# Small fp32 products of a retention layer in four quarters of TensorE, with PSUM taken in pairs of banks

## The chip, the cores and the metric

One core of one Trainium2 chip. The metric is the device time of one execution in microseconds (us), the median of several runs.

## The reference, cut to what matters

```python
# q, k, v: (4, 8, 768, 64) fp32;  w_in: (512, 2048), w_out: (2048, 512) fp64
for t in range(S):                                   # retention, per head
    state = gamma * state + k_t (outer) v_t          # 64 x 64 for each of 32 heads
    y[t] = scale * q_t @ state
x = y, heads side by side                            # (3072, 512)
h = x @ w_in;  g = h * sigmoid(h);  out = g @ w_out  # (3072, 512)
```

The kernel works in six chunks c of 128 steps for each of four batches b. One pair (c, b) is a unit, and there are 24. Inside a chunk, y is the sum of two products: masked scores times v, and q times the state that the chunks before left.

Of the kernel before, what the change touches and what calls it, by code (L numbers as in the profile page):

```python
# [12 lines left out]
FP32 = mybir.dt.float32  # L13
FP32R = mybir.dt.float32r
U32 = mybir.dt.uint32
AF = mybir.ActivationFunctionType
ALU = mybir.AluOpType
# [8 lines left out]
EPS = 2.0 ** -12  # L26
# [5 lines left out]
def kernel(  # L32
# [21 lines left out]



    nc = tc.nc
    B, H, S, D = q.shape
    DM, DF = moe_w_in.shape
    C = 128  # L60
    NC = S // C
    HP = H // 2
    KIN = DM // 128
    NF = DF // 128
    NT = B * C
# [7 lines left out]
    PS = bass.MemoryType.PSUM  # L73

    def pool(name, bufs, **kw):
        return ctx.enter_context(tc.tile_pool(name=name, bufs=bufs, **kw))
# [3 lines left out]
    xpool = pool("xpool", 2)  # L80
    const = pool("const", 1)
    ld = pool("ld", 2)
    one = pool("one", 1)
    hpool = pool("hpool", 3)
    stage = pool("stage", 2)
    conv = pool("conv", 1)
    ps_a = pool("ps_a", 4, space=PS)
    ps_h = pool("ps_h", 2, space=PS)

    g_dram = {(c, f): dram.tile([128, NT], FP32, tag=f"g{c}_{f}", name=f"gd_{c}_{f}")  # L90
# [23 lines left out]
    kqv = {"k": {}, "q": {}, "v": {}}  # L114
# [10 lines left out]



    staged = {}

    def load_w(i):  # L130
        if i >= 2 * NF:
            return
        if wide:
            t = stage.tile([128, 2 * DM], U32, tag="wf", name=f"wf_{i}")
            w_in, w_out, n = moe_w_in.bitcast(U32), moe_w_out.bitcast(U32), 256
        else:
            t = stage.tile([128, DM], FP32, tag="wf", name=f"wf_{i}")
            w_in, w_out, n = moe_w_in, moe_w_out, 128
        if i < NF:
            nc.sync.dma_start(out=t.rearrange("p (i f) -> p i f", i=KIN),  # L140
                              in_=w_in[:, ts(i, n)].rearrange("(i p) f -> p i f", p=128))
        else:
            nc.sync.dma_start(out=t, in_=w_out[ts(i - NF, 128), :])
        staged[i] = t
# [38 lines left out]
    evac, w_sb = [], {}  # L183
# [23 lines left out]
    ident = const.tile([128, 128], FP32, tag="ident", name="ident")  # L207
# [7 lines left out]
    decay = const.tile([128, 2, HP, C], FP32, tag="decay", name="decay")  # L215
# [40 lines left out]

    xt, kt, qt, am, live = {}, {}, {}, {}, {}

    def bank(name):
        return ps_a.tile([128, 512], FP32, tag="a", name=name)  # L260

    def scale_k(n):
        if 0 <= n < len(units) and units[n][0] < NC - 1:
# [9 lines left out]

    def stage_t(n):

        for name, src, to, bufs in (("k", kqv["k"][n], kt, 2), ("q", kqv["q"].pop(n), qt, 3)):
            tp = bank(f"{name}tp_{n}").rearrange("p (a t) -> p a t", a=HP)
            for a in range(HP):
                nc.tensor.transpose(tp[:, a, :], src[:, 2 * a : 2 * a + 2, :], ident)
            t = one.tile([128, HP, C], FP32, tag=f"{name}t", name=f"{name}t_{n}", bufs=bufs)  # L280
            evac[:] = [nc.scalar.copy(out=t, in_=tp).ins]
            to[n] = t

    def stage_a(n):

        ap = [bank(f"sc{j}_{n}").rearrange("p (a t) -> p a t", a=HP) for j in range(2)]
        ktn = kt.pop(n)
        for a in range(HP):
            for j in range(2):
                nc.tensor.matmul(ap[j][:, a, :], lhsT=ktn[ts(j, D), a, :],  # L290
                                 rhs=qt[n][ts(j, D), a, :], start=True, stop=True,
                                 skip_group_check=True)
        am[n] = []
        for j in range(2):
            t = one.tile([128, HP, C], FP32, tag=f"am{j}", name=f"am{j}_{n}")
            nc.vector.tensor_tensor(out=t, in0=ap[j], in1=decay[:, j], op=ALU.mult)  # L296
            am[n].append(t)

    def stage_y(n):

        c, b = units[n]
        kf, vs = kqv["k"].pop(n), kqv["v"].pop(n)
        qtn, amn = qt.pop(n), am.pop(n)
        if c < NC - 1:
            sp = bank(f"s_{n}")[:, : HP * D].rearrange("p (a e) -> p a e", a=HP)
            for a in range(HP):
                for j in range(2):
                    h = 2 * a + j
                    nc.tensor.matmul(sp[ts(j, D), a, :], lhsT=kf[:, h, :], rhs=vs[:, h, :],
                                     start=True, stop=True, skip_group_check=True)  # L310
        if b == 0 and c != LATE:
            xt[c] = xpool.tile([128, 3, KIN, NT], FP32R, tag="xt", name=f"xt_{c}")
        yp = bank(f"y_{n}").rearrange("p (a t) -> p a t", a=HP)

        if c > 0:
            for a in range(HP):
                for j in range(2):
                    nc.tensor.matmul(yp[ts(j, D), a, :], lhsT=state[b][ts(j, D), a, :],  # L318
                                     rhs=qtn[ts(j, D), a, :], start=(a == 0), stop=False,
                                     skip_group_check=True)  # L320
        for a in range(HP):
            for j in range(2):
                nc.tensor.matmul(yp[ts(j, D), a, :], lhsT=vs[:, 2 * a + j, :],  # L323
                                 rhs=amn[j][:, a, :], start=(c == 0 and a == 0), stop=True,
                                 skip_group_check=True)
        live[n] = sp if c < NC - 1 else None, yp

    def finish_y(n):
        c, b = units[n]
        sp, yp = live.pop(n)  # L330
        if c == LATE:
            y = hpool.tile([128, KIN, C], FP32, tag="hs", name=f"ys_{b}")
            nc.scalar.copy(out=y, in_=yp)
            nc.sync.dma_start(out=y_dram[b], in_=y)
        else:
            split_x(c, b, yp)
        if c == 0:
            nc.scalar.copy(out=state[b], in_=sp)
        elif c < NC - 1:
            nc.vector.tensor_tensor(out=state[b], in0=state[b], in1=sp, op=ALU.add)  # L340

    def split_x(c, b, y):
        xh, xl, xm = (xt[c][:, i, :, ts(b, C)] for i in range(3))
        nc.scalar.activation(out=xh, in_=y, func=AF.Copy, scale=HALF)
        nc.vector.tensor_tensor(out=xl, in0=y, in1=xh.bitcast(FP32), op=ALU.subtract)  # L345
        nc.vector.scalar_tensor_tensor(out=xm, in0=xl.bitcast(FP32), scalar=-1.0 / EPS,
                                       in1=xh.bitcast(FP32), op0=ALU.mult, op1=ALU.add)


    LATE = 2  # L350

    def late_x(b):
        if b == 0:
            xt[LATE] = xpool.tile([128, 3, KIN, NT], FP32R, tag="xt", name=f"xt_{LATE}")
        y = hpool.tile([128, KIN, C], FP32, tag="hs", name=f"yr_{b}")
        nc.sync.dma_start(out=y, in_=y_dram[b])
        split_x(LATE, b, y)

    visits = [0]

    def visit():
        m = visits[0]
        visits[0] += 1
        if m - 2 >= len(units):
            return
        if m < len(units):
            stage_t(m)
        if m >= 2:
            stage_y(m - 2)
        if 1 <= m <= len(units):  # L370
            stage_a(m - 1)
            scale_q(m - 1)
            scale_k(m - 1)
        if m >= 2:
            finish_y(m - 2)
        load("k", m + 2)
        load("q", m + 2)
        load("v", m)
# [77 lines left out]
    half = NF // 2  # L456
# [36 lines left out]
    for c in range(NC):  # L493
        acc = []
        for b in range(B):
            if b < 2:
                acc.append([bank(f"o{i}{b}_{c}") for i in "ab"])
            else:
                acc.append([ps_h.tile([128, DM], FP32, tag=f"h{i}", name=f"o{i}{b}_{c}")
                            for i in "ab"])  # L500
        for f in range(NF):
            n = c * NF + f
            split(n + S_AHEAD)
            t = ready.pop(n)
            first_, last = f == 0, f == NF - 1
            for b in range(B):
                gh, glo, gm = (t[:, i, ts(b, C)] for i in range(3))
                oa, ob = acc[b]
                nc.tensor.matmul(oa, lhsT=gh, rhs=wo[f][:, 0, :], start=first_, stop=False)  # L509
                nc.tensor.matmul(oa, lhsT=glo, rhs=wo[f][:, 1, :], start=False, stop=last)  # L510
                nc.tensor.matmul(ob, lhsT=gm, rhs=wo[f][:, 2, :], start=first_, stop=last)  # L511
        for b in range(B):
            oa, ob = acc[b]
            o = one.tile([128, DM], FP32, tag=("am0", "am1", "kt", "qt")[b], name=f"o_{c}_{b}",
                         bufs=(1, 1, 2, 3)[b])
            nc.scalar.activation(out=o, in_=oa, func=AF.Copy, scale=ONE_E)  # L516
            nc.vector.tensor_tensor(out=o, in0=o, in1=ob, op=ALU.subtract)  # L517
            nc.scalar.dma_start(out=out[ds(b * S + c * C, C), :], in_=o)
# [30 lines left out]
```

## The kernel before: the parts that the change and the argument touch

A *visit* is the retention work of one round: transposes of unit m, the products into y of unit m-2, the scores of unit m-1. Visits stand between the dense products (`ha`, `hb`) in TensorE's fixed order. The order of the other engines is not fixed by the program: the build picks it, and it also puts in the waits between instructions that touch the same tile. (The *build* turns the program into one list of instructions for each engine. *Masking* is VectorE's product of the scores with the decay. An *evacuation* is any reading of PSUM by ScalarE or VectorE that frees it for the next use.)

```python
ps_a = pool("ps_a", 4, space=PS)      # four single PSUM banks, taken in turn
ps_h = pool("ps_h", 2, space=PS)      # ha and hb, two each: the other four banks
...
def stage_t(n):                       # transposes; one bank for k, one for q
    for name, src, to, bufs in (("k", ...), ("q", ...)):
        tp = bank(f"{name}tp_{n}").rearrange("p (a t) -> p a t", a=HP)
        for a in range(HP):
            nc.tensor.transpose(tp[:, a, :], src[:, 2 * a : 2 * a + 2, :], ident)
        t = one.tile([128, HP, C], FP32, ...)
        evac[:] = [nc.scalar.copy(out=t, in_=tp).ins]
...
def stage_a(n):                       # scores: 64 rows by 128 columns, a bank for each j
    for a in range(HP):
        for j in range(2):
            nc.tensor.matmul(ap[j][:, a, :], lhsT=ktn[ts(j, D), a, :],
                             rhs=qt[n][ts(j, D), a, :], ...)
    for j in range(2):
        nc.vector.tensor_tensor(out=t, in0=ap[j], in1=decay[:, j], op=ALU.mult)
...
def stage_y(n):                       # s, then y of the state (64x64), then y of the scores (128x64)
    ...
        nc.tensor.matmul(sp[ts(j, D), a, :], lhsT=kf[:, h, :], rhs=vs[:, h, :], ...)
    ...
        nc.tensor.matmul(yp[ts(j, D), a, :], lhsT=state[b][ts(j, D), a, :],
                         rhs=qtn[ts(j, D), a, :], ...)
    ...
        nc.tensor.matmul(yp[ts(j, D), a, :], lhsT=vs[:, 2 * a + j, :], rhs=amn[j][:, a, :], ...)
...
def split_x(c, b, y):                 # the three parts of x: xh (ScalarE), xl and xm (VectorE)
...
def visit():
    stage_t(m); stage_y(m - 2); stage_a(m - 1); scale_q(m - 1); scale_k(m - 1); finish_y(m - 2)
```

## Time and profile before

| | before |
|---|---|
| median of 3 runs | 663.93 us |
| span of the profiled run | 661.2 us |
| TensorE, VectorE, ScalarE busy | 97%, 64%, 43% |
| one full late visit | 4.72 us |
| first late visit starts at | 173.0 us, 488.2 us before the end |

Two more lines are needed later. The first is VectorE's row of busy tenths, in 40 slices of 16.5 us; the second is a wait: who waited for whom, us in total, times, longest.

```profile
DVE  5999999985668677673447776364464554554631
...
PE qtp L279 <- DVE xt L345: 3.2, 3, 1.5
```

VectorE is full from the second slice to the eighth. In all the run, q's transposes waited three times for an evacuation of PSUM, and k's transposes not once. So four single banks, each let go by itself, were nearly enough.

### The profile page before, as it was taken

How to read it: one execution, taken by the hardware profiler on the slowest of the kernel's cores; microseconds unless marked ns; L12 is line 12 of the kernel's file. 1: busy time of each engine (PE TensorE's matmuls, PEld its weight loads, DVE VectorE, ACT ScalarE, POOL GpSimd, SP SyncE). 2: the span in 40 equal slices, each digit the busy share in tenths (PEclk: the TensorE clock that was granted, in tenths of full speed). 3: DMA queues.
4: the chain of work that ended last, by engine and by line, in shares of the span. 5: the costliest groups of instructions: out<-in, count | busy, mean ns of one | idle time of the engine just before them, and what ended most of it. 6: DMA issues, size and time to landing. Idle time of an engine off the chain costs nothing.

```text
span 661.2 us, 10308 instructions
## 1 busy us (share of the span) xinstructions
PE 639.6 (97%) x3904; PEld 525.1 (79%) x3904; DVE 424.1 (64%) x720; ACT 285.2 (43%) x510; POOL 11.1 (2%) x44
## 2 busy tenths in 40 slices
PE   4799999999999999999999999999999999999996
PEld 3578878876888888888888888888888888888885
DVE  5999999985668677673447776364464554554631
ACT  6565566645444544444447882222141312222311
POOL 3000000000000000000000000000000000000000
PEclk9999999999999999999999999999999999999999
DMA  9988878666557575754425754252343342423501
GB/s 224 207 176 200 212 211 223 208 219 210 159 153 216 180 219 160 223 168 152 128 81 160 214 184 143 65 178 80 125 131 124 121 134 85 170 86 105 160 0 64
DMA packets 122546, 103.45 MB, mean 156 GB/s; under 512 B 79488, under 2 KB 87680, under 8 KB 122496
## 3 DMA queue, kind: packets, MB, share of 16 engines
q1 hardware_dynamic: 119040, 96.49, 50.9%
q10 hardware_dynamic: 3456, 6.29, 2.6%
q8 instruction: 31, 0.51, 0.3%
q14 instruction: 19, 0.16, 0.1%
HBM read 66.06 MB, written 36.70 MB: 155 GB/s over the span
## 4 chain that ended last, share of the span: by engine, by line
PE 78%; DVE 14%; DMA 4%; issue 2%; ACT 1%; SPq 0%; DVEq 0%; ACTq 0%
PE ob L511 13%; PE oa L510 13%; PE oa L509 13%; PE ha L390 10%; PE hb L392 10%; PE ha L391 10%; PE y L323 2%; PE y L318 2%; PE sc L290 2%; DVE am L296 2%; DVE g L395 2%; DVE cp L177 1%; DVE wil L105 1%; DVE cs L173 1%; DMA vf<-in_v_dram 1%
## 5 line engine op out<-in xcount | busy, mean ns | idle before, releaser
L390 PE MATMUL ha<-xt,wi 128*128 128x512 f32 x384 | 152.2, 396 | 0.8 <-ACT g L394 0.8
L392 PE MATMUL hb<-xt,wi 128*128 128x512 f32 x384 | 150.3, 391 | 1.2 <-DVE g L395 0.8
L391 PE MATMUL ha<-xt,wi 128*128 128x512 f32 x384 | 149.8, 390 | 0.1
L511 PE MATMUL ob<-wo,gs 128*128 128x512 f32 x384 | 149.5, 389 | 0.0
L510 PE MATMUL oa<-wo,gs 128*128 128x512 f32 x384 | 149.4, 389 | 0.0
L509 PE MATMUL oa<-wo,gs 128*128 128x512 f32 x384 | 149.4, 389 | 0.0
L437 DVE TENSOR_TENSOR gs<-gr,gs 128x512 fp32r<-128x512 f32 x96 | 62.5, 686 | 92.5 <-ACT gs L435 92.5
L435 ACT ACTIVATE gs<-gr 128x512 fp32r<-128x512 f32 x96 | 53.5, 622 | 140.0 <-issue 129.6
L395 DVE TENSOR_TENSOR g<-g,hb 128x512 f32<-128x512 f32 x96 | 65.8, 685 | 67.0 <-ACT g L394 67.0
L392 PEld LDWEIGHTS hb<-xt,wi 128*128 128x128 f32 x384 | 72.1, 188 | 19.0 <-DVE g L395 3.1
L390 PEld LDWEIGHTS ha<-xt,wi 128*128 128x128 f32 x384 | 72.0, 188 | 18.8 <-ACT g L394 2.1
L394 ACT ACTIVATE g<-ha 128x512 f32<-128x512 f32 x96 | 57.1, 595 | 66.9 <-PE ha L391 62.0
L511 PEld LDWEIGHTS ob<-wo,gs 128*128 128x128 f32 x384 | 72.1, 188 | 15.8 <-DVE o L517 0.9
L510 PEld LDWEIGHTS oa<-wo,gs 128*128 128x128 f32 x384 | 72.1, 188 | 15.1
L391 PEld LDWEIGHTS ha<-xt,wi 128*128 128x128 f32 x384 | 72.1, 188 | 14.7 <-DVE xt L345 0.4
L396 ACT ACTIVATE g<-g 128x512 f32<-128x512 f32 x96 | 61.0, 636 | 52.7 <-DVE g L395 52.7
L509 PEld LDWEIGHTS oa<-wo,gs 128*128 128x128 f32 x384 | 72.1, 188 | 14.6
L438 DVE SCALAR_TENSOR_TENSOR gs<-gs 128x512 fp32r<-128x512 f32 x96 | 62.4, 686 | 0.4
L517 DVE TENSOR_TENSOR o<-o,ob 128x512 f32<-128x512 f32 x24 | 15.9, 687 | 38.9 <-ACT o L516 38.9
L516 ACT ACTIVATE o<-oa 128x512 f32<-128x512 f32 x24 | 13.7, 597 | 56.4 <-PE oa L510 49.1
L296 DVE TENSOR_TENSOR am<-sc,decay 128x512 f32<-128x512 f32 x48 | 31.5, 685 | 1.6 <-PE sc L290 1.6
L290 PE MATMUL sc<-qt,kt 64*128 64x128 f32 x384 | 28.6, 290 | 0.0
(59 smaller groups left out, 537.4 us busy)
## 6 DMA issues: line engine op xcount, KB each, us to landing
gd<-g SPq DMA_DIRECT2D x96, 256.0 KB, 3.0
gr<-gd SPq DMA_DIRECT2D x96, 256.0 KB, 2.7
wf<-in_moe_w_in_dram SPq DMA_DIRECT2D x16, 512.0 KB, 4.3
wf<-in_moe_w_out_dram SPq DMA_DIRECT2D x16, 512.0 KB, 3.9
kf<-in_k_dram SPq DMA_DIRECT2D x24, 256.0 KB, 4.7
qf<-in_q_dram SPq DMA_DIRECT2D x24, 256.0 KB, 5.0
vf<-in_v_dram SPq DMA_DIRECT2D x24, 256.0 KB, 4.1
out_dram<-o ACTq DMA_DIRECT2D x24, 256.0 KB, 2.1
```

The source lines that it names most:

```text
L390: nc.tensor.matmul(ha, lhsT=w[0], rhs=x[0], start=first_, stop=False)
L391: nc.tensor.matmul(ha, lhsT=w[1], rhs=x[1], start=False, stop=last)
L392: nc.tensor.matmul(hb, lhsT=w[2], rhs=x[2], start=first_, stop=last)
L394: nc.scalar.activation(out=hs, in_=ha, func=AF.Copy, scale=ONE_E)
L395: nc.vector.tensor_tensor(out=hs, in0=hs, in1=hb, op=ALU.subtract)
L396: nc.scalar.activation(out=hs, in_=hs, func=AF.Silu)
L435: nc.scalar.activation(out=t[:, 0, :], in_=g, func=AF.Copy, scale=HALF)
L437: nc.vector.tensor_tensor(out=t[:, 1, :], in0=g, in1=high, op=ALU.subtract)
L438: nc.vector.scalar_tensor_tensor(out=t[:, 2, :], in0=t[:, 1, :].bitcast(FP32), scalar=-1.0 / EPS, in1=high, op0=ALU.mult, op1=ALU.add)
L509: nc.tensor.matmul(oa, lhsT=gh, rhs=wo[f][:, 0, :], start=first_, stop=False)
L510: nc.tensor.matmul(oa, lhsT=glo, rhs=wo[f][:, 1, :], start=False, stop=last)
L511: nc.tensor.matmul(ob, lhsT=gm, rhs=wo[f][:, 2, :], start=first_, stop=last)
```

## The change

Its intent: fill all four 64 by 64 quarters of the array in the product of q and the state, and keep the array in one shape for as long as possible. For that it

- issues s, y of the scores, y of the state, scores, in that order, so that equal shapes are neighbours;
- sends the odd head pairs of y to the crossed quarters and to a second bank. This exchanges halves of x, so the rows of the first weights are loaded exchanged too, in three transfers in place of one;
- computes the scores as twice as many 64 by 64 products;
- takes PSUM in pairs of banks. Two pairs, in place of four single banks, serve in turn: a pair for k's and q's transposes, the next for y and s, the next for the scores, which are then masked by one VectorE operation of 1024. The accumulators and result buffers of the output stage follow suit;
- splits y ahead of the masking in the program, and makes the third part of x (`xm`) after it.

```diff
-    ps_a = pool("ps_a", 4, space=PS)
+    ps_u = pool("ps_u", 2, space=PS)
...
+            nc.sync.dma_start(out=to[0], in_=src[0])
+            for j in range(2):
+                nc.sync.dma_start(out=to[1, ts(j, D)], in_=src[1, ts(1 - j, D)])
...
+    def banks(name):
+        return ps_u.tile([128, 2, 512], FP32, tag="u", name=name)
...
     def stage_t(n):
-        for name, src, to, bufs in (("k", kqv["k"][n], kt, 2), ("q", kqv["q"].pop(n), qt, 3)):
-            tp = bank(f"{name}tp_{n}").rearrange("p (a t) -> p a t", a=HP)
+        tp = banks(f"tp_{n}")
+        for i, (name, src, to, bufs) in enumerate((("k", kqv["k"][n], kt, 2),
+                                                   ("q", kqv["q"].pop(n), qt, 3))):
+            part = tp[:, i].rearrange("p (a t) -> p a t", a=HP)
             for a in range(HP):
-                nc.tensor.transpose(tp[:, a, :], src[:, 2 * a : 2 * a + 2, :], ident)
+                nc.tensor.transpose(part[:, a, :], src[:, 2 * a : 2 * a + 2, :], ident)
             t = one.tile([128, HP, C], FP32, tag=f"{name}t", name=f"{name}t_{n}", bufs=bufs)
-            evac[:] = [nc.scalar.copy(out=t, in_=tp).ins]
+            evac[:] = [nc.scalar.copy(out=t, in_=part).ins]
...
+        for a in range(HP):                                # y of the scores, now first
+            for j in range(2):
+                o = j ^ (a % 2)
+                product(o, a % 2, out=yp[ts(o, D), a // 2, a % 2, :], ...)
+        if c > 0:                                          # y of the state, four quarters
+            for i in range(0, HP, 2):
+                for a in (i, i + 1):
+                    for j in range(2):
+                        o = j ^ (a % 2)
+                        product(o, a % 2, out=yp[ts(o, D), a // 2, a % 2, :],
+                                lhsT=state[b][ts(j, D), a, :], rhs=qtn[ts(j, D), a, :], stop=True)
...
+                for half in range(2):                      # scores in four quarters
+                    nc.tensor.matmul(u[ts(half, D), j, a, :], lhsT=ktn[ts(j, D), a, ts(half, D)], ...)
...
         if m >= 2:
             stage_y(m - 2)
+            rest = finish_y(m - 2)
         if 1 <= m <= len(units):
             stage_a(m - 1)
             scale_q(m - 1)
             scale_k(m - 1)
-        if m >= 2:
-            finish_y(m - 2)
+        if rest is not None:
+            rest()                                         # xm
```

More of the change, by code (lines that the diff above doesn't have):

```diff
@@ L139, in load_w @@
         if i < NF:
-            nc.sync.dma_start(out=t.rearrange("p (i f) -> p i f", i=KIN),
-                              in_=w_in[:, ts(i, n)].rearrange("(i p) f -> p i f", p=128))
+            to = t.rearrange("p (i o f) -> o p i f", o=2, f=n)
+            src = w_in[:, ts(i, n)].rearrange("(i o p) f -> o p i f", o=2, p=128)
+            nc.sync.dma_start(out=to[0], in_=src[0])
+            for j in range(2):
+                nc.sync.dma_start(out=to[1, ts(j, D)], in_=src[1, ts(1 - j, D)])
         else:
@@ L257 @@
     xt, kt, qt, am, live = {}, {}, {}, {}, {}
-    def bank(name):
-        return ps_a.tile([128, 512], FP32, tag="a", name=name)
+    def banks(name):
+        return ps_u.tile([128, 2, 512], FP32, tag="u", name=name)
     def scale_k(n):
@@ L280, in stage_t, with stage_y, product @@
             t = one.tile([128, HP, C], FP32, tag=f"{name}t", name=f"{name}t_{n}", bufs=bufs)
-            evac[:] = [nc.scalar.copy(out=t, in_=tp).ins]
+            evac[:] = [nc.scalar.copy(out=t, in_=part).ins]
             to[n] = t
+    def stage_y(n):
+        c, b = units[n]
+        kf, vs = kqv["k"].pop(n), kqv["v"].pop(n)
+        qtn, amn = qt[n], am.pop(n)
+        u = banks(f"y_{n}")
+        yp = u[:, :, : 2 * C].rearrange("p o (i t) -> p i o t", i=2)
+        sp = u[:, 1, 2 * C :].rearrange("p (a e) -> p a e", a=HP)
+        started = set()
+        def product(j, bank, **kw):
+            nc.tensor.matmul(start=(j, bank) not in started, skip_group_check=True, **kw)
+            started.add((j, bank))
+        if c < NC - 1:
+            for a in range(HP):
+                for j in range(2):
+                    h = 2 * a + j
+                    product(j, 1, out=sp[ts(j, D), a, :], lhsT=kf[:, h, :], rhs=vs[:, h, :],
+                            stop=True)
+        for a in range(HP):
+            for j in range(2):
+                o = j ^ (a % 2)
+                product(o, a % 2, out=yp[ts(o, D), a // 2, a % 2, :], lhsT=vs[:, 2 * a + j, :],
+                        rhs=amn[:, j, a, :], stop=(c == 0))
+        if c > 0:
+            for i in range(0, HP, 2):
+                for a in (i, i + 1):
+                    for j in range(2):
+                        o = j ^ (a % 2)
+                        product(o, a % 2, out=yp[ts(o, D), a // 2, a % 2, :],
+                                lhsT=state[b][ts(j, D), a, :], rhs=qtn[ts(j, D), a, :],
+                                stop=True)
+        live[n] = sp, yp
@@ L284, in stage_a @@
     def stage_a(n):
-        ap = [bank(f"sc{j}_{n}").rearrange("p (a t) -> p a t", a=HP) for j in range(2)]
+        u = banks(f"sc_{n}").rearrange("p j (a t) -> p j a t", a=HP)
         ktn = kt.pop(n)
@@ L289, in stage_a @@
             for j in range(2):
-                nc.tensor.matmul(ap[j][:, a, :], lhsT=ktn[ts(j, D), a, :],
-                                 rhs=qt[n][ts(j, D), a, :], start=True, stop=True,
-                                 skip_group_check=True)
-        am[n] = []
-        for j in range(2):
-            t = one.tile([128, HP, C], FP32, tag=f"am{j}", name=f"am{j}_{n}")
-            nc.vector.tensor_tensor(out=t, in0=ap[j], in1=decay[:, j], op=ALU.mult)
-            am[n].append(t)
-    def stage_y(n):
-        c, b = units[n]
-        kf, vs = kqv["k"].pop(n), kqv["v"].pop(n)
-        qtn, amn = qt.pop(n), am.pop(n)
-        if c < NC - 1:
-            sp = bank(f"s_{n}")[:, : HP * D].rearrange("p (a e) -> p a e", a=HP)
-            for a in range(HP):
-                for j in range(2):
-                    h = 2 * a + j
-                    nc.tensor.matmul(sp[ts(j, D), a, :], lhsT=kf[:, h, :], rhs=vs[:, h, :],
-                                     start=True, stop=True, skip_group_check=True)
-        if b == 0 and c != LATE:
-            xt[c] = xpool.tile([128, 3, KIN, NT], FP32R, tag="xt", name=f"xt_{c}")
-        yp = bank(f"y_{n}").rearrange("p (a t) -> p a t", a=HP)
-        if c > 0:
-            for a in range(HP):
-                for j in range(2):
-                    nc.tensor.matmul(yp[ts(j, D), a, :], lhsT=state[b][ts(j, D), a, :],
-                                     rhs=qtn[ts(j, D), a, :], start=(a == 0), stop=False,
-                                     skip_group_check=True)
-        for a in range(HP):
-            for j in range(2):
-                nc.tensor.matmul(yp[ts(j, D), a, :], lhsT=vs[:, 2 * a + j, :],
-                                 rhs=amn[j][:, a, :], start=(c == 0 and a == 0), stop=True,
-                                 skip_group_check=True)
-        live[n] = sp if c < NC - 1 else None, yp
+                for half in range(2):
+                    nc.tensor.matmul(u[ts(half, D), j, a, :], lhsT=ktn[ts(j, D), a, ts(half, D)],
+                                     rhs=qt[n][ts(j, D), a, :], start=True, stop=True,
+                                     skip_group_check=True)
+        am[n] = one.tile([128, 2, HP, C], FP32, tag="am", name=f"am_{n}")
+        nc.vector.tensor_tensor(out=am[n], in0=u, in1=decay, op=ALU.mult)
     def finish_y(n):
@@ L330, in finish_y @@
         sp, yp = live.pop(n)
+        qt.pop(n)
+        if b == 0 and c != LATE:
+            xt[c] = xpool.tile([128, 3, KIN, NT], FP32R, tag="xt", name=f"xt_{c}")
         if c == LATE:
             y = hpool.tile([128, KIN, C], FP32, tag="hs", name=f"ys_{b}")
-            nc.scalar.copy(out=y, in_=yp)
+            nc.scalar.copy(out=y.rearrange("p (i o) t -> p i o t", o=2), in_=yp)
             nc.sync.dma_start(out=y_dram[b], in_=y)
+            rest = None
         else:
-            split_x(c, b, yp)
+            rest = split_x(c, b, yp)
         if c == 0:
@@ L340, in finish_y @@
             nc.vector.tensor_tensor(out=state[b], in0=state[b], in1=sp, op=ALU.add)
+        return rest
     def split_x(c, b, y):
-        xh, xl, xm = (xt[c][:, i, :, ts(b, C)] for i in range(3))
+        xh, xl, xm = (xt[c][:, i, :, ts(b, C)].rearrange("p (i o) t -> p i o t", o=2)
+                      for i in range(3))
         nc.scalar.activation(out=xh, in_=y, func=AF.Copy, scale=HALF)
         nc.vector.tensor_tensor(out=xl, in0=y, in1=xh.bitcast(FP32), op=ALU.subtract)
-        nc.vector.scalar_tensor_tensor(out=xm, in0=xl.bitcast(FP32), scalar=-1.0 / EPS,
-                                       in1=xh.bitcast(FP32), op0=ALU.mult, op1=ALU.add)
+        return lambda: nc.vector.scalar_tensor_tensor(
+            out=xm, in0=xl.bitcast(FP32), scalar=-1.0 / EPS, in1=xh.bitcast(FP32),
+            op0=ALU.mult, op1=ALU.add)
     LATE = 2
@@ L356, in late_x @@
         nc.sync.dma_start(out=y, in_=y_dram[b])
-        split_x(LATE, b, y)
+        split_x(LATE, b, y.rearrange("p (i o) t -> p i o t", o=2))()
     visits = [0]
@@ L367, in visit @@
             stage_t(m)
+        rest = None
         if m >= 2:
             stage_y(m - 2)
+            rest = finish_y(m - 2)
         if 1 <= m <= len(units):
@@ L496 @@
             if b < 2:
-                acc.append([bank(f"o{i}{b}_{c}") for i in "ab"])
+                u = banks(f"o{b}_{c}")
+                acc.append([u[:, i] for i in range(2)])
             else:
@@ L513 @@
             oa, ob = acc[b]
-            o = one.tile([128, DM], FP32, tag=("am0", "am1", "kt", "qt")[b], name=f"o_{c}_{b}",
-                         bufs=(1, 1, 2, 3)[b])
+            o = one.tile([128, DM], FP32, tag=("kt", "qt")[b % 2], name=f"o_{c}_{b}",
+                         bufs=(2, 3)[b % 2])
             nc.scalar.activation(out=o, in_=oa, func=AF.Copy, scale=ONE_E)
```

## The prediction

> **What bounds the kernel now.** I read the page's totals first, then the busy time by stretches, then the waits, then one visit of the retention part in the order of time.
>
> ```profile
> PE 639.6 (97%) x3904; PEld 525.1 (79%) x3904; DVE 424.1 (64%) x720; ACT 285.2 (43%) x510; POOL 11.1 (2%) x44
> ```
>
> TensorE looks like the bound, but 97% is an average over stages. The stretches (us, then busy us of PE, PEld, DVE, ACT, POOL, the clock, the DMA share, GB/s):
>
> ```profile
> 24.00:116.00 92.00, 87.98 (x878) 72.32 (x878) 91.15 (x170) 55.40 (x97) 2.40 (x2) 1.00 0.84 204
> 116.00:156.00 40.00, 38.97 (x169) 31.13 (x168) 32.50 (x59) 21.91 (x38) 0.00 (x0) 1.00 0.69 224
> 156.00:445.00 289.00, 288.65 (x1804) 237.63 (x1804) 182.65 (x303) 142.10 (x246) 2.71 (x2) 1.00 0.53 164
> 445.00:661.20 216.20, 211.11 (x931) 174.00 (x929) 102.41 (x165) 51.01 (x92) 0.00 (x0) 0.99 0.33 107
> ```
>
> From 24 to 116 us VectorE is busy 91.15 of 92 us: it is full, and TensorE, at 87.98, only nearly so. From 156 us on VectorE is at 63% (182.65 of 289), TensorE at 99.9%. So a microsecond of TensorE is worth a microsecond after 156 us and much less before 116 us. The retention work comes in "visits" (transposes, state product s, the two products into y, the scores sc) between the dense products ha and hb. One visit of the later stage (start us, length us, engine, line, what):
>
> ```profile
> 204.47 0.60 PE L279 MATMUL ktp<-ident,kf 128*128 128x128 f32 x4
> 204.91 0.60 PE L279 MATMUL qtp<-ident,qf 128*128 128x128 f32 x4
> 205.44 0.69 PE L309 MATMUL s<-vf,kf 128*64 128x64 f32 x16
> 206.05 1.09 PE L318 MATMUL y<-qt,state 64*64 64x128 f32 x16
> 207.07 1.09 PE L323 MATMUL y<-am,vf 128*64 128x128 f32 x16
> 208.10 1.16 PE L290 MATMUL sc<-qt,kt 64*128 64x128 f32 x16
> 209.19 0.50 PE L390 MATMUL ha<-xt,wi 128*128 128x512 f32 x1
> ```
>
> The starts are what counts: a group costs the distance to the next start, so s 0.61, y of the state 1.02, y of the scores 1.02, sc 1.09, and the visit 4.72 us (204.47 to 209.19). Each of the eight products of a group shows as two records. Four whole-array transposes start in 0.44 us, 0.11 each, for 128 columns of fp32. Sixteen records at 0.11 would be 1.76 us; y of the state takes 1.02. So two already run side by side, in eight steps of 0.11 = 0.88 us, and some 0.14 is left over. What that is, the waits tell (us in total, times, longest):
>
> ```profile
> PEld sc L290 <- issue: 4.3, 24, 0.3
> PEld y L323 <- issue: 3.4, 20, 0.2
> PEld s L309 <- issue: 2.2, 13, 0.2
> ```
>
> Before sc the weight load stands idle 4.3 / 24 = 0.18 us every time, before y of the scores 3.4 / 20 = 0.17, with nothing to wait for. These are the places where the shape in the array changes: 128*64, 64*64, 128*64, 64*128 down the visit.
>
> **What the Trainium skill says.** "TensorEngine Tiling (Array Packing)", section Key Properties: changing the tiling mode, as opposed to the tile, drains TensorE. The 0.17 and 0.18 us above agree. "TensorE: Matmul & The Clock Gate", Part 3, section "Measured speedup vs the span model": products in different tiles of the array start about 4 ns apart and run together, up to 16 of them. The trace agrees for two (0.88 in place of 1.76 us); it has no case of four. The tiling page's Gotcha 1, PSUM Pressure: different row tiles must not write the same PSUM bank at once. That is why the change sends even and odd head pairs to two banks; nothing in the trace tests it. "VectorE: DVE Perf Modes", section "The DRAIN you can't avoid", says that each VectorE operation pays a flush before the next and that it is the count of operations that matters. In the trace the part that does not scale is small, as these rows show:
>
> ```profile
> 51.37 0.42 DVE L340 TENSOR_TENSOR state<-state,s 128x256 f32<-128x256 f32 x1
> 51.70 0.69 DVE L173 SCALAR_TENSOR_TENSOR cs<-ca,cs 128x512 uint32<-128x512 uint32 x1
> 52.31 0.69 DVE L345 TENSOR_TENSOR xt<-y,xt 128x512 fp32r<-128x512 f32 x1
> 52.91 0.42 DVE L175 TENSOR_SCALAR cp<-cs 128x512 uint32<-128x512 uint32 x1
> ```
>
> 256 elements take 0.33 us start to start, 512 take 0.60: 0.27 per 256, and 0.06 fixed.
>
> **The change part by part.** I take a group apart as: opening (the first pair waits for its weights, 0.05 us, for sc with its wider weights 0.1), steps, and closing (the drain into another shape, 0.09 beyond a step).
>
> Order of the visit: now s (128*64), y of the state (64*64), y of the scores (128*64), sc (64*128), dense. After: s and y of the scores, both 128*64, then y of the state and sc, both 64*64, then dense. Of the four changes of shape after s begins (s to y, y to y, y to sc, sc to dense) two stay. The two that go are s to y of the state, 0.09 + 0.05 = 0.14 us, and y of the scores to sc, 0.09 + 0.1 = 0.19 us. Together 0.33 us.
>
> y of the state: 64-row by 64-column products now use two quarters of the array on the diagonal. With the odd pairs crossed over, four quarters are filled, so 16 records take four steps in place of eight: 4 x 0.11 = 0.44 us saved, or 0.33 if the two records of a product and the order of issue cost one further step. I take 0.38.
>
> Scores: twice the products (64 columns of weights in place of 128), so 32 records in four quarters: eight steps of 0.11 as before. The array was already full. I expect 0 here beyond the drain that is counted above, perhaps minus 0.05 us for an extra step.
>
> Sum for a full visit: 0.33 + 0.38 - 0.03 = 0.68 us, 4.72 to about 4.04. After 156 us there are twelve visits: ten with transposes, y and sc (6.8 us together), one with y and sc (0.6), one with y alone (0.4). 7.8 us, one for one, for there the product after a visit waits for nothing but TensorE.
>
> VectorE: two score maskings of 512 become one of 1024: 0.06 us saved a unit, 24 units. Some ten or eleven fall where VectorE is full: 0.7 us. ACT's work does not change.
>
> Before 116 us lie eight more visits with y of the state. Their 8 x 0.68 = 5.4 us shorten TensorE where VectorE sets the pace, so TensorE will wait for it instead; I count 0.5 us of it, from the last one.
>
> PSUM: four single banks become two double ones. Their turn comes round at the same places of the visit, but a tile is free only when all its readers are done: k's transposes must wait for y's split as q's do now. In the late visits everything was read long before. In the early ones it can cost tenths, partly made good because y is split ahead of the masking. In the output stage, the first two accumulators move to double banks too; they end 2.0 and 1.4 us before the chunk's end (three products per block, each 0.23 us from start to start in the timeline), so the coarser release should not show.
>
> Weights of the first product: one transfer becomes three, 32 more issues at about 0.4 us on SP, and the first of them lie at the start, where the chain passes through them:
>
> ```profile
> 0.75 0.44 SPq L140 DMA_DIRECT2D wf<-in_moe_w_in_dram  x1
> 8.03 0.39 SPq L140 DMA_DIRECT2D wf<-in_moe_w_in_dram  x1
> 10.08 2.32 SPq L123 DMA_DIRECT2D vf<-in_v_dram  x1
> ```
>
> Bytes and packets stay the same, and the first stretch is limited by bytes rather than issues (the DMA engines are 90% busy in the first two slices of the page). I allow 0.4 us lost.
>
> Sum: 7.8 + 0.7 + 0.5 - 0.4 = 8.6 us; 663.9 - 8.6 = 655.3.
>
> **The rivals.** First, the saving before 116 us counts too. For it: TensorE runs those visits without gaps as well, at the same 4.72 us. Against it: VectorE's 99%. If it were so, 5 us more would come off: 650.5, just over 2%. Second, four quarters do not run four at a time: TensorE's instruction rate limits. In four quarters a record and its weight load must issue every 0.11 / 4 = 0.027 us. The s group shows 0.029 (0.61 less the 0.14 of opening and closing, over 16 records, and its 64 columns explain that by themselves), so the needed rate is a little beyond what is shown. If issue took 0.035, sc would grow by 0.24 us in each visit and y of the state would save 0.1 less; the gain would fall to about 5 us, 659. Third, the coarser PSUM tiles and the new order of VectorE's work open gaps in its full stretch; with a chain y, ACT, VectorE, transpose, copy, sc, masking round two visits, 0.3 us in each of ten visits would cost 3 us: 658. Fourth, the startup loses 2 us because the v load stands behind two further issues: 657.
>
> **Range and chances.** The 7.8 us rest on counted steps and removed drains and hold within about 2 us. The early stage can go 3 us either way. So 655.3, range 651.5 to 659.5. The line of faster by over 2% is 650.7, which needs the first rival nearly whole; slower would need a loss of more than 20 us against the sum, and no view offers one.
>
> **What would show it.** Right: late visits of about 4.0 us; y of the state near 0.5 to 0.6 us and sc about 1.0; the idle of the weight load by issue gone before sc and before y of the scores and present before y of the state; masking ops of about 1.2 us; the stretch to 116 us shorter by no more than 1 to 2 us, VectorE still full there and TensorE less busy. Wrong: sc over 1.2 us (second rival), VectorE idle between 24 and 116 us (third), the first s later by over 1 us (fourth), or the dense products of the late stage spaced wider than now, which would mean another wait had taken the drains' place.

## The result, and the profile after

686.32 us median of 4 runs against 663.95 for the kernel before. The ratio is 1.0333, 95% interval 1.0316 to 1.0351. (A ratio is the mean time of one kernel's runs over that of the other's runs of the same rounds, so not quite the ratio of the medians.) The change is 22 us slower; 655.3 had been predicted.

The changed kernel's total line, then two of its stretches (us, busy us of PE, PEld, DVE, ACT, POOL, the granted clock, the DMA share, GB/s):

```profile
PE 639.4 (94%) x4288; PEld 520.8 (76%) x4288; DVE 427.9 (63%) x696; ACT 284.4 (42%) x510; POOL 10.6 (2%) x44
```

```profile
24.00:116.00 92.00, 74.44 (x877) 58.94 (x876) 81.33 (x136) 47.18 (x82) 1.36 (x1) 0.93 0.67 167
...
156.00:445.00 289.00, 281.86 (x1980) 230.53 (x1979) 180.64 (x288) 144.99 (x251) 2.72 (x2) 1.00 0.55 168
```

TensorE's busy time is what it was (639.4 for 639.6), although its products got shorter, as shown below; the loss shows as idle time. From 24 to 116 us VectorE is no longer full: 81.33 us for 91.15. TensorE fell from 87.98 to 74.44. The late stretch too has 7 us of idle TensorE, where it had 0.35. One late visit of the changed kernel (start us, length us, engine, line, what, and in brackets the idle time before it and what ended it):

```profile
208.71 0.60 PE L287 MATMUL tp<-ident,kf 128*128 128x128 f32 x4
209.98 0.66 PE L287 MATMUL tp<-ident,qf 128*128 128x128 f32 x4 [0.68 <-ACT kt L289]
210.57 0.69 PE L305 MATMUL y<-vf,kf 128*64 128x64 f32 x16
211.08 1.05 PE L305 MATMUL y<-am,vf 128*64 128x128 f32 x16
212.06 0.67 PE L305 MATMUL y<-qt,state 64*64 64x128 f32 x16
212.55 1.05 PE L336 MATMUL sc<-qt,kt 64*64 64x128 f32 x32
213.53 0.50 PE L413 MATMUL ha<-xt,wi 128*128 128x512 f32 x1
```

Everything below the second row went as hoped. From start to start, s takes 0.51 us (0.61 before), y of the scores 0.98 (1.02), y of the state 0.49 (1.02) and the scores 0.98 (1.09). But q's transposes start 1.27 us after k's, where they had started 0.44 after them, and the bracket names the culprit: `kt`, ScalarE's copy of k out of PSUM. The visit is 4.82 us long in place of 4.72. What ScalarE did meanwhile:

```profile
208.72 0.60 ACT L417 ACTIVATE g<-ha 128x512 f32<-128x512 f32 x1 [0.74 <-PE ha L414]
209.34 0.59 ACT L289 COPY kt<-tp 128x512 f32<-128x512 f32 x1
```

k's transposes end at 209.31 (208.71 and 0.60), and at that moment ScalarE has just finished another evacuation. The copy then took 0.59 us, and only after it q's transposes began. Over the whole run the waits (us in total, times, longest):

```profile
PE tp L287 <- ACT kt L289: 22.4, 24, 2.8
...
PE tp L287 <- ACT state L356: 4.0, 2, 3.1
```

24 waits for 24 units. It is one wait per visit, about 0.7 us late in the run, where ScalarE comes to the copy at once, and up to 2.8 us early. The view did not have this row before. That its sum is about the whole loss is only a hint; sums of waits and time lost need not agree.

Where the loss arises, by the start of the first late visit's transposes and the time from there to the end:

| kernel | first late visit | from there to the end |
|---|---|---|
| before | 173.0 | 488.2 |
| changed | 192.86 | 490.6 |

19.9 us are lost in the early stage and 2.4 in the late one. In the early stage there is a second cost, which comes along with the idling. The two groups at the end of this piece of the changed kernel's timeline run at half speed:

```profile
39.39 1.12 PE L305 MATMUL y<-vf,kf 128*64 128x64 f32 x16
40.30 1.92 PE L305 MATMUL y<-am,vf 128*64 128x128 f32 x16
```

1.12 and 1.92 us, for 0.69 and 1.05 in the late visit, just after 3 us of waiting; from 39.3 to 42.5 us the granted clock is 0.50. The mean clock granted from 24 to 116 us is 0.93; it was 1.00. "TensorE: Matmul & The Clock Gate", Part 1, ties the granted clock to how busy TensorE has been; that agrees with what is seen here. As an estimate, 0.07 of the 92 us, 6 to 7 us of TensorE's time, is the most that the lower clock can have cost in this stretch; no run takes it away alone.

### The profile page after: what moved, and what is told of

It reads as the page before. It is cut to its first block, busy times and chain, and to the rows that moved or that the text cites. A ratio compares the mean times of both kernels' runs of the same rounds, so it can differ in the third digit from the quotient of the medians.

```text
span 683.5 us, 11097 instructions
## 1 busy us (share of the span) xinstructions
PE 639.4 (94%) x4288; PEld 520.8 (76%) x4288; DVE 427.9 (63%) x696; ACT 284.4 (42%) x510; POOL 10.6 (2%) x44
## 2 busy tenths in 40 slices
DMA packets 123061, 103.50 MB, mean 151 GB/s; under 512 B 80000, under 2 KB 88192, under 8 KB 123008
## 4 chain that ended last, share of the span: by engine, by line
PE 79%; DVE 9%; ACT 5%; DMA 3%; issue 2%; SPq 1%; ACTq 0%; DVEq 0%
PE ha L413 11%; PE ha L414 11%; PE hb L415 11%; PE ob L535 6%; PE o L533 6%; PE o L535 6%; PE o L534 6%; PE oa L533 6%; PE oa L534 6%; PE y L305 5%; PE sc L336 2%; PE tp L287 2%; DMA wf<-in_moe_w_in_dram 2%; ACT kt L289 1%; DVE g L418 1%
## 5 line engine op out<-in xcount | busy, mean ns | idle before, releaser
L535 PE MATMUL ob<-wo,gs 128*128 128x512 f32 x192 | 75.3, 392 | 0.0
L533 PE MATMUL o<-wo,gs 128*128 128x512 f32 x192 | 74.8, 389 | 0.0
L533 PE MATMUL oa<-wo,gs 128*128 128x512 f32 x192 | 74.8, 389 | 0.0
L535 PE MATMUL o<-wo,gs 128*128 128x512 f32 x192 | 74.7, 389 | 0.0
L534 PE MATMUL oa<-wo,gs 128*128 128x512 f32 x192 | 74.7, 389 | 0.0
L534 PE MATMUL o<-wo,gs 128*128 128x512 f32 x192 | 74.7, 389 | 0.0
L535 PEld LDWEIGHTS ob<-wo,gs 128*128 128x128 f32 x192 | 36.0, 188 | 8.9 <-DVE o L541 1.5
L535 PEld LDWEIGHTS o<-wo,gs 128*128 128x128 f32 x192 | 36.0, 188 | 7.6
L534 PEld LDWEIGHTS oa<-wo,gs 128*128 128x128 f32 x192 | 36.1, 188 | 7.5
L534 PEld LDWEIGHTS o<-wo,gs 128*128 128x128 f32 x192 | 36.0, 188 | 7.5
```

The lines of the kernel that those rows point to most:

```text
L533: nc.tensor.matmul(oa, lhsT=gh, rhs=wo[f][:, 0, :], start=first_, stop=False)
L534: nc.tensor.matmul(oa, lhsT=glo, rhs=wo[f][:, 1, :], start=False, stop=last)
L535: nc.tensor.matmul(ob, lhsT=gm, rhs=wo[f][:, 2, :], start=first_, stop=last)
```

## The experiments

Three theories were told apart. **A**: q's transposes wait for k's copy because both lie in one PSUM tile. **B**: a pair is let go only when all its readers are done, so k's transposes wait for more than before. **C**: the weight loads in three pieces starve the start. A fourth, that the new products themselves or their order disturb the early stage, was added with the later runs.

### Copies after both sets of transposes

```diff
             for a in range(HP):
                 nc.tensor.transpose(part[:, a, :], ...)
-            t = one.tile(...)
-            evac[:] = [nc.scalar.copy(out=t, in_=part).ins]
+            parts.append((name, to, bufs, part))
+        for name, to, bufs, part in parts:
+            t = one.tile(...)
+            evac[:] = [nc.scalar.copy(out=t, in_=part).ins]
```

In the built program this one move takes a wait off q's first transpose. Two lines of the listing of TensorE's instructions, the changed kernel above, this one below:

```
L287 Matmult tp_262<-ident,qf_209 128x128 [waits DMAHW4_49,Activation_49]
L287 Matmult tp_262<-ident,qf_209 128x128 [waits DMAHW4_49]
```

The q transposes of all 24 units lose this wait. So the wait on ScalarE comes from the build, for a write to bank 1 of a tile after a read of bank 0 of it. The kernel before, with two tiles, has no such wait.

> The changed kernel, with the transposes of k and of q issued first and the two ScalarE copies out of the pair of banks after both. Theory A (q's transposes wait for k's copy because both lie in one PSUM tile): the idle of 0.68 us before q's transposes goes, late visits fall from 4.82 to about 3.9 us, the early stage recovers most of its 20 us, total 655 to 663 us. Theory B (the pair is released only when all its readers are done, so k's transposes wait for the state copy and the split): late visits fall to 3.9 too but the early stage keeps most of its loss, total 672 to 677. Theory C (the weight loads in three pieces starve the start): early stage unchanged, total 674 or more.

Measured: 670.1 us, correct, ratio to the kernel before 1.0099 (1.0084 to 1.0114). 16.2 us of the 22 are back. A late visit:

```profile
200.01 0.60 PE L287 MATMUL tp<-ident,kf 128*128 128x128 f32 x4
200.44 0.60 PE L287 MATMUL tp<-ident,qf 128*128 128x128 f32 x4
200.97 0.69 PE L307 MATMUL y<-vf,kf 128*64 128x64 f32 x16
...
203.94 0.50 PE L415 MATMUL ha<-xt,wi 128*128 128x512 f32 x1
```

The 0.43 us from k's transposes to q's are back, and the visit is 3.93 us long. The first late visit starts at 185.02 us and the end comes 483.1 us later. So the wait cost 7.8 us of the early stage (192.86 less 185.02) and 7.5 of the late one (490.6 less 483.1). The wait is theory A's. But the total lies between what A and B expect, and the early stage got back 7.8 of its 19.9 us where A expected most of it: A is not all. The largest wait of TensorE for another engine is now that of the scores for q's copy, six times in the early visits, where it was 2.1 us in three times before this edit:

```profile
PE sc L338 <- ACT qt L291: 7.8, 6, 2.3
```

No run takes this wait away alone, so its share of the remaining loss stays open.

### Pairs of banks alone, in the kernel before

```diff
-    ps_a = pool("ps_a", 4, space=PS)
+    ps_u = pool("ps_u", 2, space=PS)
     ... # k and q, s and y, the two score banks: halves of a pair each; all else as before
```

> The kernel before with nothing changed but PSUM: four single banks become two pairs (k and q, s and y, the two score banks), copies between the transposes as in the changed kernel. Theory A and B: much slower than before, 675 to 690 us, with q's transposes idle about 0.7 us before each late visit. Theory C, or a fault in the new products: within 3 us of the kernel before, 661 to 667.

Measured: 686.5 us, correct, ratio 1.0351 (1.0334 to 1.0369): slower than before by about as much as the whole change, with none of its products, loads or order. Its late visit and its wait:

```profile
202.83 0.60 PE L282 MATMUL tp<-ident,kf 128*128 128x128 f32 x4
204.10 0.66 PE L282 MATMUL tp<-ident,qf 128*128 128x128 f32 x4 [0.68 <-ACT kt L284]
```

```profile
PE tp L282 <- ACT kt L284: 18.9, 24, 1.9
```

The same 0.68 us, the same 24 waits. PSUM's grouping alone is enough for a slowdown of this size. That the two totals agree so well is chance: from the first late visit on, the changed kernel takes 7.6 us less than this one (490.6 for 498.2), thanks to its products, and before it 6.7 us more (first late visit at 192.86 for 186.19), for which the loads and `xm` are looked at below.

### Pairs of banks with copies last, in the kernel before

The edit is the two above together.

> The kernel before with pairs of banks, and both copies after all transposes. Theory A: within 4 us of the kernel before, 662 to 668. Theory B: still 8 us or more slower than before, as the pair is still released as one. Late visits 4.7 us under both.

Measured: 672.08 us, correct, ratio 1.0132 (1.0117 to 1.0147). Of the 23 us that pairs cost, 14.4 are the wait on k's copy (686.5 less 672.08). 8.6 remain with no such wait, as theory B expects (8 or more). Late visits are 4.72 us and the end comes 489.1 us after the first of them, about as before (488.2); the first late visit starts at 180.59. So these 8.6 us are nearly all lost in the early stage. Two of its waits:

```profile
PE tp L282 <- ACT state L344: 4.6, 3, 2.4
...
PE hb L398 <- DVE xt L352: 3.7, 1, 3.7
```

k's transposes wait for the state copy, which shares its pair with y (in the kernel before they never waited for an evacuation), and the first dense product waits 3.7 us for `xm` (0.4 before).

### One transfer for each slice of the weights

```diff
-            nc.sync.dma_start(out=to[0], in_=src[0])
-            for j in range(2):
-                nc.sync.dma_start(out=to[1, ts(j, D)], in_=src[1, ts(1 - j, D)])
+            nc.sync.dma_start(out=t.rearrange("p (i f) -> p i f", i=KIN), in_=...)
```

on top of the copies-last kernel; the result is wrong, since x stays exchanged.

> As the changed kernel with copies last, but each slice of the first weights in one transfer, without the exchange of halves, so the result is wrong on purpose. Theory C: 3 us or more faster than the copies-last kernel. Theory A and B: within 2 us of it, the first s of the states about 1 us earlier.

Measured: 668.39 us, 1.7 less than the copies-last kernel (ratios 1.0073 and 1.0099 to the same runs of the kernel before). The first s starts at 16.54 us in place of 18.32. The transfers cost 1.7 us; theory C as stated (3 us or more) does not hold.

### The state copy ahead of the split, twice

In the pairs kernel the built program made ScalarE's copy of the state wait for VectorE's reading of y in the same pair.

```diff
         else:
+            if c == 0:
+                nc.scalar.copy(out=state[b], in_=sp)
             split_x(c, b, yp)
-        if c == 0:
-            nc.scalar.copy(out=state[b], in_=sp)
-        elif c < NC - 1:
+        if 0 < c < NC - 1:
             ... # the state's sum on VectorE, as before
```

> The kernel before with pairs of banks and copies last, and the first chunk's state copy on ScalarE ahead of the split of y, so that it no longer waits for VectorE's read of the same pair. If the 8.6 us that are left with pairs come from readers of one pair being put in a row (state copy behind the split, k's transposes behind both), half or more of it goes: 664 to 668 us. If they come from the pair's release as such (transposes behind the split whatever the order), it stays at 670 to 673.

> The same move in the changed kernel with copies last (670.1 us). Readers in a row: 663 to 667. Release as such: 669 to 671.

Measured: 672.88 us (ratio 1.0146) in the pairs kernel, and 671.17 (1.0121) in the changed kernel with copies last. Neither is faster than without the move. k's transposes now wait for the split in place of the state copy, and no shorter (5.9 us in all for 4.6 in the pairs kernel, 4.4 for 4.1 in the changed one). So the order of the readers is not the cost. That a pair waits for its last reader fits both runs, but no run takes away that wait alone.

### The third part of x right after the second

```diff
-            rest = split_x(c, b, yp)
+            split_x(c, b, yp)()
+            rest = None
```

> As the one before, and the third part of x is made right after the second on VectorE, not after the masking and scaling. If the dense product that waits for that third part (2.5 us at the chunk changes, and the first one) is what is left of the loss, 3 us or more faster than the one before. If it is covered elsewhere, within 2 us of it.

Measured: 666.93 us, ratio 1.0056 (1.0041 to 1.0071), 4.2 us less than the kernel without this move. The dense product's wait for `xm` fell from 3.5 us to this:

```profile
PE hb L418 <- DVE xt L369: 1.2, 1, 1.2
```

Deferring `xm` was a loss of its own, of some 4 us in this setting.

### The split ahead of the masking, in the kernel before with pairs

```diff
             stage_y(m - 2)
+            finish_y(m - 2)
         if 1 <= m <= len(units):
             ...
-        if m >= 2:
-            finish_y(m - 2)
```

> The kernel before with pairs and copies last (672.1 us), with y's split and its third part ahead of the masking in program order. If what is left of the pairs' loss lies in the order in which VectorE gets the third part of x (the first dense product waited 3.7 us for it), 666 to 669. If it lies in the transposes that wait for a whole pair, 671 to 673.

Measured: 669.83 us, ratio 1.0095 (1.0076 to 1.0114). That is 2.3 us better than the pairs kernel with copies last, and it lies between the two expectations. The wait for `xm` before the first `hb` fell from 3.7 to 0.7 us, but the first dense product itself starts 3.1 us later (40.81 for 37.68). I could not separate further how much of the 8.6 us is the order of VectorE's work and how much the transposes' waits.

### A pair for y alone

```diff
-    ps_u = pool("ps_u", 2, space=PS)
+    ps_u = pool("ps_u", 1, space=PS)       # y and s
+    ps_a = pool("ps_a", 2, space=PS)       # k, q and the two score banks, in turn
```

with the changed kernel's products and loads, the state copy ahead of the split and `xm` at once as in the run that made the third part right after the second, and two maskings of 512 again.

> The changed kernel's products and loads, with a pair of banks for y alone and single banks for k, q and the two score banks (two maskings of 512 again), third part of x right after the second. If pairs are the cost and not the new products, the early stage loses no more than 3 us on the kernel before and the late visits stay at about 3.9 us: 656 to 662. If the early stage suffers from the new products or loads as such, 664 to 668.

Measured: 671.8 us, correct, ratio 1.0131 (1.0112 to 1.0149). A miss: late visits are 3.93 us as expected, but the early stage lost more than with pairs. The wait moved:

```profile
PE ktp L289 <- DVE am L343: 11.9, 7, 2.5
```

Only two single banks are left, so k's transposes now wait until the scores of the visit before are masked by the engine that is full. The number of PSUM tiles that can be let go independently does not decide by itself: here there are three, and with two pairs the same products, loads and order of `xm` took 666.93 us. What counts is for which reader, on which engine, the next write has to wait.

### TensorE's order alone, in the kernel before

Four single banks, loads and masking as before; s, y of the scores, y of the state on the diagonal, scores in quarters.

```diff
+        for a in range(HP): ...            # y of the scores first
         if c > 0:
             for a in range(HP): ...        # then y of the state
...
+                for half in range(2):
+                    nc.tensor.matmul(ap[j][ts(half, D), a, :], lhsT=ktn[ts(j, D), a, ts(half, D)], ...)
```

> The kernel before with its four single banks, its loads and its masking; only TensorE's order changes: s, y of the scores, y of the state, scores in 64 by 64 quarters. If two drains a visit are worth 0.33 us and nothing else is lost, late visits 4.72 to about 4.4, twelve of them 4 us, total 658 to 660.5. If the new order alone disturbs the early stage, 663 or more. That sc costs no more in 32 records than in 16 shows as 0.9 to 1.0 us from its first start to the next dense product.

Measured: 663.4 us, correct, ratio 1.0005 (0.999 to 1.0021). Late visits fell to 4.35 us, but the early stage gave it all back. The first of them starts at 176.9 us (173.0 before). With TensorE's new instructions the build put the other engines' instructions in another order: from the 61st VectorE instruction on it differs from the kernel before.

### The same from the thirteenth unit on

```diff
+        if n < LATE_UNIT:                  # 12: the order and the scores of the kernel before
...
+        else:                              # the regrouped order, scores in quarters
```

> The kernel before, with the regrouped order and the scores in quarters only from the thirteenth unit on, so that the stage where VectorE is full keeps its instructions and their order. If the late visits' 0.37 us are real and the regrouped kernel lost them again through the early stage's order, twelve visits give about 4 us: 659 to 660. If something late eats them, 662 to 664.

Measured: 659.14 us (5 runs), correct, ratio 0.9941 (0.9927 to 0.9954): faster than both kernels. A late visit:

```profile
203.03 0.60 PE L281 MATMUL ktp<-ident,kf 128*128 128x128 f32 x4
203.46 0.60 PE L281 MATMUL qtp<-ident,qf 128*128 128x128 f32 x4
203.99 0.69 PE L313 MATMUL s<-vf,kf 128*64 128x64 f32 x16
204.51 1.05 PE L334 MATMUL y<-am,vf 128*64 128x128 f32 x16
...
207.38 0.50 PE L407 MATMUL ha<-xt,wi 128*128 128x512 f32 x1
```

No pair, no wait. The visit is 4.35 us long, the first late one starts at 172.29 us (173.0 before) and the end comes 484.8 us after it (488.2 before). VectorE's first 269 instructions, and all of ScalarE's, stand in the order of the kernel before. Together with the run above it shows that the late gain is real, and that the same instructions in the early stage are no gain; that it is the other engines' order that costs there is the likely cause, not shown by itself.

## Why the prediction was wrong, point by point

**The step that failed** is the paragraph on PSUM: "Their turn comes round at the same places of the visit, but a tile is free only when all its readers are done", "In the late visits everything was read long before", "In the early ones it can cost tenths". I asked when a pair is let go to the next user, and not what happens inside one pair. k's and q's transposes share one; between them in the program stands a read of it, k's copy, and the build makes the second write wait for that read. Taking it away brought back 16.2 us in the changed kernel (copies last) and 14.4 in the kernel before with pairs. The diff showed it: `evac` inside the loop over k and q, now on halves of one tile. "No view offers one" was said of a loss of 20 us; but the views were those of the kernel before, which has no such wait.

**The early release** was seen as a rival (the third, 3 us) and mis-sized: pairs with copies last cost 8.6 us, of which the split ahead of the masking brought back 2.3. The reading that led there was half right. VectorE was full from 24 to 116 us, so a faster TensorE gains little there; but then a slower feed costs time there, and VectorE's busy time in that stretch fell from 91.15 to 81.33 us.

**`xm` after the masking** I passed over: the split "ahead of the masking" was counted as a help. 4.2 us came back when the deferral was undone.

**The startup** was put at 0.4 us. The loads cost 1.7, so the fourth rival (2 us) was close, and its sign is there: the first s starts at 18.92 us for 16.46. The packets did not stay the same either (122546 before, 123061 after).

**The products** were right, almost to the number. Two drains gone, y of the state at 0.49 us ("0.5 to 0.6"), the scores at 0.98 ("about 1.0") and twice the records at no cost. The runs separate the two parts: two changes of shape fewer are worth 0.37 us (4.72 to 4.35, regrouped; 0.33 predicted), and four quarters a further 0.42 (4.35 to 3.93; 0.38 predicted). The second rival, TensorE's rate of instructions, falls: 32 records of the scores take no longer than 16 did. A full late visit without the wait is 3.93 us for 4.04 predicted. The stretch from the first late visit to the end shrank by 5.1 us (488.2 to 483.1) for the 7.8 summed up. The twelve visits themselves shrank by 7.4 us (51.1 to 43.8 together), although some of them wait up to 0.35 us for q's copy. The rest was lost outside them: 1.2 us between the visits, nearly all of it at two places where a dense product waits for VectorE's `g`, and 1.0 after the last visit.

**Coarser release in the output stage**, "should not show", shows a little: from the end of the last visit to the end of the run it is 315.7 us before, and 316.6 to 316.8 in every kernel with two pairs.

**Two readings of the lines** were too simple. The list of idle weight loads has no row for y of the state, although the shape changes there too (128\*64 to 64\*64): the trace shows 0.07 us at that place, for 0.17 at the two others. And the trace of the kernel before does test the rule on row tiles and banks: in y of the state, products from the upper and the lower 64 rows start 7 ns apart and write the two halves of the partitions of one bank, and the results are correct. So the rule as cited is too wide where the halves differ.

**The signs that I named** did work. "VectorE idle between 24 and 116 us (third)" is what the changed kernel's stretches show first.

## What to carry to other kernels

When buffers are merged into a larger tile, list every write and read of it in program order and look for a read that stands between two writes to different parts: the build may order them even where they touch different banks. (In the kernel before, the copy out of k's bank and q's transposes into another ran side by side, from 205.11 to 205.51 us.) Ask of each write for which reader of the same buffer it must wait, and on which engine; where an engine is full and its feed goes round such a ring of buffers, a merged buffer can turn into idle time of that engine. And try a gain in the stage where its engine sets the pace, leaving the other stages' instructions alone: here that turned the regrouped order, without the pairs and the crossed quarters, from no gain (663.4 us) into one of 0.6% (659.14).

## What the Trainium skill lacked or had wrong

- "TensorEngine Tiling (Array Packing)", Key Properties, says that a change of tiling mode drains TensorE but gives no duration. Here the weight load stands idle 0.17 to 0.18 us at two such places in a visit and 0.07 at a third, and two places fewer in a visit are worth 0.37 us (4.72 to 4.35, the regrouped kernels).
- "TensorE: Matmul & The Clock Gate", Part 3, lists measured packings of 4, 3, 9 and 16 tiles. It has none for fp32 in four 64 by 64 quarters: 16 records in 0.49 us and 32 in 0.98. With no change of shape between them, y of the state and the scores together take 1.47 us, against 1.89 with y on the diagonal in two quarters (regrouped).
- "PSUM — Partial Sum Buffer", section "PSUM bank collisions raise a hardware error", says to guard PSUM by bank and quadrant. No page says that a tile over two banks is ordered as one by the build: a read of one bank held a write to the other for 0.68 us in each late visit, and without it the run was 16.2 us shorter.
- No page says that TensorE's instructions alone can change the order that the build gives to the other engines. Regrouping them throughout was worth nothing (663.4 us against 663.2), and only late 4.0 us.
